# Normalising token blocks where they are read instead of where they are stored

## The chip, the core and the metric

One core of a Trainium2 chip runs the whole program. The metric is device time in microseconds from launch to end; the median of three runs of the kernel before is 2909.83 us (2909.57 to 2911.71). TensorE (PE) does the matmuls, VectorE (DVE) and ScalarE (ACT) the elementwise work and the evacuation of PSUM, GpSimd (POOL) some additions and a DMA queue, SyncE (SP) the main DMA queue. SBUF is the on-chip memory, PSUM holds the matmul results, HBM is off the chip.

## What is computed

Three layers on float32 data, 4 batches of 3072 tokens with 256 channels:

```python
X = np.fft.fft(np.fft.fft(x, axis=1), axis=2).real      # mixes tokens and channels
h = np.maximum(X @ w_in, 0.0)                           # 1024 wide
u, v = h[..., :512], h[..., 512:]
mu = np.mean(v, axis=-1, keepdims=True)
var = np.mean((v - mu) ** 2, axis=-1, keepdims=True)
v_n = (v - mu) / np.sqrt(var + 1e-06)                   # per token
v_s = np.einsum('ts,bsd->btd', w_spatial, v_n) + b_spatial[None, :, None]
y = (u * v_s) @ w_out                                   # 256 wide
gate = 1.0 / (1.0 + np.exp(-(y @ w_gate)))
out = (gate * (y @ w_val)) @ w_out2
```

The change concerns `v_n`: the scale 1/sqrt(var + 1e-6) and the shift -mu * scale of every token.

## The kernel before

Every float32 operand of a matmul is kept as a rounded high part and the remainder, the low part, and a product is three matmuls (`mm3`, L257 to L261: high x high, high x low, low x high).

**The front** (up to 321 us of the trace). Per batch, POOL folds the input `xt` by its symmetries (`fold_half`, `fold_x`, L371 and L372, `folds`), ACT and POOL split the folded tiles (`split_fold`, L254, L255), and PE transforms them along the tokens (`fft`, `psf`). The result, in four units a batch, feeds blocks of 128 tokens: `v_block` (a tile of 128 tokens x 512, and its mirror image) and `u_block` (128 channels of `u`). The order is written out by hand: a global `step` counts the blocks, 116 in all, 29 per batch, seven or eight per unit. A block's second matmuls come two steps after its first (`LAG = 2`), its third part one step later. Each unit needs a small tile `nt` that ACT makes from `nts` (`own_samples`, L592) at the last block of the unit before.

For a token tile `tv` ACT takes the Relu (L634, L640), DVE subtracts for the mirror image (`mirror`, L612) and takes the statistics (L642). After the last block of a unit come, one step each: `ln1` (aggregate, L673, L674), `root` (a square root on ACT, L677), `ln2` (L682 to L688: a Newton step, then `y`, the scale, and `nm`, the shift; `yp` lies in PSUM, in the pool of `lnb`), and three `norms` steps, which normalise two tiles each in place (`norm`, L693 on DVE or L697 on ACT by `NORM_ON`) and then store them to `v_d` in HBM (`store`, L703 to L709); unit 3 has one odd row in a tile of its own. A `u` tile goes from PSUM to `tu` (L660, L612) and to `u_d` (L665). The stores are issued on SP, those of the last batch on POOL. The tiles `tv` have 13 buffers, `tu` three.

At step 100 (`FIRST`) the program frees the tables of the front and starts to load blocks of the next stage (`start_a`), and at steps 106, 109, 113 and 115 (`NEXT`) it prepares the first four jobs (`prepare_next`).

**The spatial product** (321 to 1805 us). `w_spatial` times `v_n` is done with seven products of half-size blocks instead of eight (Strassen's scheme, `V_OF`, `W_OF`): for two pairs of batches `p`, seven products `i`, three column groups `c`, 42 leaves; each leaf has six steps `kp` of 24 matmuls. A job prepares one operand of one step: `load_job` brings one or two blocks of [128, 2, 512] from `v_d` or from the weights into `st` buffers (seven of them), `prepare_job` adds or subtracts the two where the scheme says so (L781, DVE), ACT casts the high part (L785), DVE takes the low part (L788, put off to the next job). There are 252 weight jobs and 84 token jobs; the token jobs of the next product run in the third leaf of the one before. `advance` prepares three steps ahead (`LEAD`) and loads two further.

**The second layer** (1805 us to the end) is not touched.

## Time and profile before

| what | value |
|---|---|
| median of the runs | 2909.83 us |
| span of the profiled execution | 2908.4 us |
| PE busy, of the span | 2832.1 us, 97% |
| DVE, ACT, POOL busy | 2039.4, 1341.2, 226.6 us |
| mean granted clock of TensorE, whole span | 0.991 |

The profile shows one execution. A busy PE is not PE at its peak, since overlapping matmuls count as one busy stretch; the number of matmuls in a stretch and the granted clock tell more. The time of a run is to be compared with other runs, the span with stretches of the same trace. Lines are those of the kernel before.

### The profile page before, as it was taken

How to read it: one execution, taken by the hardware profiler on the slowest of the kernel's cores; microseconds unless marked ns; L12 is line 12 of the kernel's file. 1: busy time of each engine (PE TensorE's matmuls, PEld its weight loads, DVE VectorE, ACT ScalarE, POOL GpSimd, SP SyncE). 2: the span in 40 equal slices, each digit the busy share in tenths (PEclk: the TensorE clock that was granted, in tenths of full speed). 3: DMA queues.
4: the chain of work that ended last, by engine and by line, in shares of the span. 5: the costliest groups of instructions: out<-in, count | busy, mean ns of one | idle time of the engine just before them, and what ended most of it. 6: DMA issues, size and time to landing. Idle time of an engine off the chain costs nothing.

```text
span 2908.4 us, 33957 instructions
## 1 busy us (share of the span) xinstructions
PE 2832.1 (97%) x12550; PEld 2355.8 (81%) x12550; DVE 2039.4 (70%) x2971; ACT 1341.2 (46%) x2151; POOL 226.6 (8%) x332
## 2 busy tenths in 40 slices
PE   5998799999999999999999999999999999999999
PEld 4887688888888888888888888888888888888887
DVE  7887775787766666577667476866677667766665
ACT  4888433233233232233223233666556556565655
POOL 2882100011100001000000000000000000000000
PEclk8999899999999999999999999999999999999999
DMA  6676866787756777587777485200000000000000
GB/s 227 241 257 237 320 236 202 267 312 264 261 200 212 263 248 255 177 287 256 246 257 242 147 278 169 82 34 29 30 3 27 30 30 30 15 15 30 29 15 15
DMA packets 148135, 470.75 MB, mean 162 GB/s; under 512 B 16753, under 2 KB 18289, under 8 KB 147584
## 3 DMA queue, kind: packets, MB, share of 16 engines
q1 hardware_dynamic: 140528, 434.88, 43.6%
q0 software_dynamic: 3984, 21.11, 1.8%
q10 hardware_dynamic: 3456, 12.58, 1.1%
q8 instruction: 98, 1.61, 0.2%
q14 instruction: 69, 0.57, 0.1%
HBM read 385.94 MB, written 82.58 MB: 161 GB/s over the span
## 4 chain that ended last, share of the span: by engine, by line
PE 92%; DVE 3%; ACT 2%; issue 1%; DMA 1%; POOL 0%; ACTq 0%; SPq 0%; DVEq 0%; POOLq 0%
PE bank L259 29%; PE bank L260 29%; PE bank L261 29%; DMA u_d<-tu 1%; PE psf L259 1%; PE psf L261 0%; PE psf L260 0%; PE psu L261 0%; PE psv L259 0%; PE psu L259 0%; PE psu L260 0%; PE psv L260 0%; PE psv L261 0%; DVE stats L642 0%; ACT tu L660 0%
## 5 line engine op out<-in xcount | busy, mean ns | idle before, releaser
L259 PE MATMUL bank<-wh,vh 128*128 128x512 f32 x2016 | 785.4, 390 | 6.7 <-DVE nm L688 6.7
L260 PE MATMUL bank<-wl,vh 128*128 128x512 f32 x2016 | 785.1, 389 | 0.0
L261 PE MATMUL bank<-wh,vl 128*128 128x512 f32 x2016 | 784.9, 389 | 0.0
L788 DVE TENSOR_TENSOR wl<-st,wh 128x1024 fp32r<-128x1024 f32 x252 | 311.3, 1235 | 430.9 <-ACT wh L785 427.6
L785 ACT CAST wh<-st 128x1024 fp32r<-128x1024 f32 x252 | 265.8, 1055 | 677.4 <-PE bank L261 442.5
L259 PEld LDWEIGHTS bank<-wh,vh 128*128 128x128 f32 x2016 | 379.0, 188 | 85.8 <-DVE nm L688 7.4
L261 PEld LDWEIGHTS bank<-wh,vl 128*128 128x128 f32 x2016 | 379.0, 188 | 79.0
L260 PEld LDWEIGHTS bank<-wl,vh 128*128 128x128 f32 x2016 | 379.0, 188 | 78.5
L781 DVE TENSOR_TENSOR st<-st 128x1024 f32<-128x1024 f32 x240 | 293.4, 1223 | 16.7 <-DMA st<-in_wt 11.6
L259 PE MATMUL bank<-x,wgh 128*128 128x512 f32 x673 | 262.4, 390 | 0.5 <-ACT t L1290 0.4
L1278 DVE TENSOR_TENSOR t<-t,bank 128x512 f32<-128x512 f32 x144 | 99.0, 688 | 233.5 <-PE bank L261 233.5
L260 PE MATMUL bank<-x,wgh 128*128 128x512 f32 x673 | 261.8, 389 | 0.0
L261 PE MATMUL bank<-x,wgl 128*128 128x512 f32 x673 | 261.8, 389 | 0.0
L1299 DVE TENSOR_TENSOR gl<-s,gh 128x512 fp32r<-128x512 f32 x288 | 199.5, 693 | 57.7 <-ACT gh L1297 44.4
L259 PE MATMUL bank<-gh,wv 128*128 128x512 f32 x576 | 224.2, 389 | 0.8 <-ACT gh L1292 0.8
L260 PE MATMUL bank<-gl,wv 128*128 128x512 f32 x576 | 224.2, 389 | 0.2 <-DVE gl L1299 0.2
L261 PE MATMUL bank<-gh,wv 128*128 128x512 f32 x576 | 224.1, 389 | 0.0
L1269 ACT ACTIVATE s<-s 128x512 f32<-128x512 f32 x144 | 91.1, 633 | 153.3 <-DVE s L1268 153.3
L259 PEld LDWEIGHTS bank<-x,wgh 128*128 128x128 f32 x673 | 126.3, 188 | 28.5 <-ACT s L1266 0.9
L1070 ACT COPY x<-bank 128x512 f32<-128x512 f32 x48 | 28.3, 589 | 259.2 <-PE bank L261 259.2
L261 PEld LDWEIGHTS bank<-x,wgl 128*128 128x128 f32 x673 | 126.4, 188 | 26.1
L260 PEld LDWEIGHTS bank<-x,wgh 128*128 128x128 f32 x673 | 126.4, 188 | 26.0
(232 smaller groups left out, 4467.8 us busy)
## 6 DMA issues: line engine op xcount, KB each, us to landing
st<-in_wt SPq DMA_DIRECT2D x432, 512.0 KB, 5.3
st<-v_d SPq DMA_DIRECT2D x144, 512.0 KB, 4.9
u<-u_d SPq DMA_DIRECT2D x96, 256.0 KB, 4.3
u_d<-tu SPq DMA_DIRECT2D x48, 384.0 KB, 3.3
v_d<-tv SPq DMA_DIRECT2D x69, 256.0 KB, 2.4
xt<-in_xh SPq DMA_DIRECT2D x24, 512.0 KB, 4.3
x_d<-x ACTq DMA_DIRECT2D x24, 512.0 KB, 2.7
raw<-x_d SPq DMA_DIRECT2D x24, 512.0 KB, 4.1
```

The costliest lines, as they stand in the source:

```text
L259: nc.tensor.matmul(out=ps, lhsT=w[0], rhs=x[0], start=first, stop=False, **kw)
L260: nc.tensor.matmul(out=ps, lhsT=w[0], rhs=x[1], start=False, stop=False, **kw)
L261: nc.tensor.matmul(out=ps, lhsT=w[1], rhs=x[0], start=False, stop=last, **kw)
L781: nc.vector.tensor_tensor(out=tiles[0], in0=tiles[0], in1=tiles[1], op=ALU.add if sign > 0 else ALU.subtract)
L785: nc.scalar.copy(hl[0], tiles[0])
L788: lows.append(lambda: nc.vector.tensor_tensor(out=hl[1], in0=tiles[0], in1=f(hl[0]), op=ALU.subtract))
L1070: nc.scalar.copy(side["x2"][:, o, :], ps)
L1269: nc.scalar.activation(s1, s1, AF.Sigmoid)
L1278: nc.vector.tensor_tensor(out=g["t2"], in0=g["t2"], in1=g["b"], op=ALU.add)
L1299: nc.vector.tensor_tensor(out=l, in0=s, in1=f(h), op=ALU.subtract)
```

## The change

Token tiles go to `v_d` as they are after the Relu, right after their statistics (`store` in `rest` and in `only`). `norm`, `norms`, `last_norm`, `NORM_ON` and the entries that followed `ln2` are gone. `ln2` writes scale and shift of all token tiles into one tile `ln_of` that stays in SBUF; the odd row of unit 3 is put there by an eight-byte DMA. In the spatial product `norm_job` applies scale and shift with two ACT operations per token job (to the second block where a job has two, with the shifts of both blocks combined), and `prepare_job` multiplies the first block by its scale in the same DVE operation that adds the second. `advance` issues `norm_job` for all jobs that are due before it prepares them. The pools change: `tv` from 13 buffers to nine, `tu` from three to five.

```diff
@@ -304,6 +304,9 @@
 
 
     r0, l0, f0 = ExitStack(), ExitStack(), ExitStack()
+    lnp = pool(ctx, "lnp", 1, "right")
+    ln_of = lnp.tile([P, B * 24, 2], F32, name="ln_of")
+    shifts = {}
     keep = pool(r0, "keep", 1, "right")
     pqp = pool(r0, "pqp", 2, "right")
     cst = pool(l0, "cst", 1)
@@ -580,8 +583,8 @@
         take_nyquist(*fft(fold_n, B, unit, 0, early=True), unit)
     s0.close()
     stp = pool(r0, "stp", 2, "right")
-    vp = pool(r0, "vp", 13, "right")
-    up = pool(r0, "up", 3, "right")
+    vp = pool(r0, "vp", 9, "right")
+    up = pool(r0, "up", 5, "right")
 
     lnb = ps_l.tile([P, 2, 8], F32, name="lnb")
     nt_of = {}
@@ -603,7 +606,7 @@
         tiles = {}
         stats = stp.tile([P, 7, 6], F32, name="stats")
         mv = stp.tile([P, 7, 2], F32, name="mv")
-        ve, sd, y, nm = (stp.tile([P, 7], F32, name=n) for n in ("ve", "sd", "y", "nm"))
+        ve, sd = (stp.tile([P, 7], F32, name=n) for n in ("ve", "sd"))
         yp = lnb[:, unit % 2, :]
 
 
@@ -622,7 +625,12 @@
                 tv = vp.tile([P, DH], F32, tag="tv", name="tv")
                 nc.scalar.activation(tv, ps, AF.Relu)
                 tiles[6] = tv
-                return lambda: lambda: nc.vector.bn_stats(stats[:, 6, :], tv)
+
+                def only():
+                    nc.vector.bn_stats(stats[:, 6, :], tv)
+                    store(6)
+
+                return lambda: only
             ev = stp.tile([P, DH], F32, tag="e", name="ev", bufs=4)
             nc.scalar.copy(ev, ps)
 
@@ -640,6 +648,7 @@
                 nc.scalar.activation(tv, tv, AF.Relu)
                 for sg in range(2):
                     nc.vector.bn_stats(stats[:, sg * 3 + m, :], tiles[sg * 3 + m])
+                    store(sg * 3 + m)
 
             return second
 
@@ -684,17 +693,17 @@
             stt(out=ve[:, a], in0=yp[:, a], scalar=-0.5, in1=ve[:, a], op0=ALU.mult, op1=ALU.mult)
             nc.vector.tensor_tensor(out=ve[:, a], in0=ve[:, a], in1=yp[:, a], op=ALU.mult)
             stt(out=yp[:, a], in0=ve[:, a], scalar=1.5, in1=yp[:, a], op0=ALU.add, op1=ALU.mult)
-            nc.vector.tensor_copy(y[:, a], yp[:, a])
-            stt(out=nm[:, a], in0=mv[:, a, 0], scalar=-1.0, in1=yp[:, a], op0=ALU.mult, op1=ALU.mult)
-
-        def norm(i):
-            tv = tiles[i]
-            if NORM_ON[i] != "a":
-                engines[NORM_ON[i]].tensor_scalar(
-                    out=tv, in0=tv, scalar1=y[:, i : i + 1], scalar2=nm[:, i : i + 1], op0=ALU.mult, op1=ALU.add
-                )
-            else:
-                nc.scalar.activation(tv, tv, AF.Identity, scale=y[:, i : i + 1], bias=nm[:, i : i + 1])
+            at = b * 24 + unit * 6
+            places = [(slice(0, 6), ln_of[:, at : at + 6, :])]
+            if nb == 7:
+                own = stp.tile([P, 1, 2], F32, name="own")
+                places.append((slice(6, 7), own))
+            for k, to in places:
+                nc.vector.tensor_copy(to[:, :, 0], yp[:, k])
+                stt(out=to[:, :, 1], in0=mv[:, k, 0], scalar=-1.0, in1=yp[:, k], op0=ALU.mult, op1=ALU.mult)
+            if nb == 7:
+                q = H - (R3 - P)
+                queue.dma_start(ln_of[0:1, at + 3 : at + 4, :], own[q : q + 1, :, :])
 
         def store(i):
             tv = tiles[i]
@@ -708,23 +717,12 @@
             else:
                 queue.dma_start(v_d[b][:, unit * 6 + i, :], tv)
 
-        def norms(i):
-            for k in (i, i + 3):
-                norm(k)
-            for k in (i, i + 3):
-                store(k)
-
-        def last_norm():
-            norm(6)
-            store(6)
-
         blocks = []
         for i in range(4):
             if i < nb - 3:
                 blocks.append(lambda i=i: v_block(i))
             blocks.append(lambda i=i: u_block(i))
-        after = [root, ln2] + [lambda i=i: norms(i) for i in range(3)] + ([last_norm] if nb == 7 else [])
-        return blocks, [ln1] + after
+        return blocks, [ln1, root, ln2]
 
 
     la, ls, ra, pa_ = ExitStack(), ExitStack(), ExitStack(), ExitStack()
@@ -773,14 +771,52 @@
                 tiles.append(st)
         staged[n] = tiles
 
+    def columns(p, block):
+        at = (2 * p + block[0]) * 24 + 12 * block[1]
+        return ln_of[:, at : at + 12, :]
+
+    def shift_of(p, i):
+
+        first, second, sign = V_OF[i]
+        if second is None:
+            return columns(p, first)[:, :, 1]
+        if (p, i) not in shifts:
+            shifts[p, i] = lnp.tile([P, 12], F32, name=f"shift{p}{i}")
+            nc.vector.tensor_tensor(
+                out=shifts[p, i],
+                in0=columns(p, second)[:, :, 1],
+                in1=columns(p, first)[:, :, 1],
+                op=ALU.add if sign > 0 else ALU.subtract,
+            )
+        return shifts[p, i]
+
+    def norm_job(n):
+
+        _, kind, key = jobs[n]
+        if kind == "v":
+            p, i, kp = key
+            first, second, _ = V_OF[i]
+            st, scale, shift = staged[n][-1], columns(p, second or first)[:, :, 0], shift_of(p, i)
+            for k in range(2):
+                at = slice(2 * kp + k, 2 * kp + k + 1)
+                nc.scalar.activation(st[:, k, :], st[:, k, :], AF.Identity, scale=scale[:, at], bias=shift[:, at])
+
     def prepare_job(n):
         _, kind, key = jobs[n]
         sign = (V_OF if kind == "v" else W_OF)[key[1]][2]
         tiles = staged.pop(n)
-        if sign:
-            nc.vector.tensor_tensor(
-                out=tiles[0], in0=tiles[0], in1=tiles[1], op=ALU.add if sign > 0 else ALU.subtract
-            )
+        op = ALU.add if sign > 0 else ALU.subtract
+        if sign and kind == "v":
+            p, i, kp = key
+            scale = columns(p, V_OF[i][0])[:, :, 0]
+            for k in range(2):
+                at = slice(2 * kp + k, 2 * kp + k + 1)
+                st = tiles[0][:, k, :]
+                nc.vector.scalar_tensor_tensor(
+                    out=st, in0=st, scalar=scale[:, at], in1=tiles[1][:, k, :], op0=ALU.mult, op1=op
+                )
+        elif sign:
+            nc.vector.tensor_tensor(out=tiles[0], in0=tiles[0], in1=tiles[1], op=op)
         hl = [A[kind].tile([P, 2, 512], F32R, tag=kind + i, name=kind + i) for i in "hl"]
         nc.scalar.copy(hl[0], tiles[0])
 
@@ -802,7 +838,11 @@
     def advance(step, loads):
 
         load_due(step + loads)
-        while state["prep"] < len(jobs) and jobs[state["prep"]][0] <= step:
+        due = state["prep"]
+        while due < len(jobs) and jobs[due][0] <= step:
+            norm_job(due)
+            due += 1
+        while state["prep"] < due:
             prepare_job(state["prep"])
             state["prep"] += 1
 
@@ -814,21 +854,20 @@
         load_due(1)
 
     def prepare_next():
+        norm_job(state["prep"])
         prepare_job(state["prep"])
         state["prep"] += 1
         load_job(state["load"])
         state["load"] += 1
 
     units = [(b, unit) for b in range(B) for unit in (3, 2, 0, 1)]
-    LAG, NORM_DVE = 1, (0, 1, 2, 3, 4, 5, 6)
-
 
 
     FOLDS, SPLITS, SPLIT_ON = (-3, 1, 4, 8, 13, 13), (17, 19, 23), "ppp"
     AT3, AT2, AT0, END0 = (26, 28), (2, 6), (11, 13), (10, 12)
     FIRST, NEXT = 100, (106, 109, 113, 115)
-    LAG, NORM_ON, NYQ = 2, "avavava", 4
-    engines = {"v": nc.vector, "p": nc.gpsimd}
+    LAG, NYQ = 2, 4
+    engines = {"p": nc.gpsimd}
     plan = {}
     folds_of, parts_of = {b: [] for b in range(B)}, {0: fold, B: fold_n}
     parts_of.update({b: [] for b in range(1, B)})
```

## Rows read from the trace of the kernel before

**Rows 1.** Busy by stretch: us of PE, PEld, DVE, ACT, POOL (instructions), clock, DMA, GB/s.

```profile
56.00:280.00 224.00, 206.27 (x1018) 185.20 (x1019) 182.97 (x455) 186.99 (x377) 150.59 (x233) 0.98 0.62 223
280.00:321.00 41.00, 22.21 (x89) 18.18 (x88) 29.62 (x80) 25.17 (x49) 13.61 (x25) 0.75 0.82 309
321.00:1805.00 1484.00, 1484.00 (x6539) 1228.33 (x6540) 1015.92 (x1147) 448.61 (x518) 48.57 (x54) 1.00 0.71 243
1805.00:2908.00 1103.00, 1097.94 (x4836) 906.93 (x4834) 762.10 (x1169) 659.37 (x1169) 0.00 (x0) 1.00 0.08 28
```

**Rows 2.** Waits of PE, 56 to 321 us: total us, times, longest us.

```profile
PE psv L620 <- ACT nt L592: 18.0, 7, 7.3
PE bank L259 <- DVE nm L688: 6.7, 1, 6.7
...
PE psu L259 <- ACT eu L654: 3.8, 3, 3.1
```

**Rows 3.** Busy time by stretch, the ten us ahead of a hot spot and in it.

```profile
90.00:100.00 10.00, 10.00 (x52) 9.04 (x51) 8.00 (x20) 9.49 (x20) 9.84 (x16) 1.00 0.88 319
100.00:110.00 10.00, 7.36 (x29) 6.21 (x28) 9.86 (x20) 9.81 (x20) 8.36 (x12) 0.83 0.41 160
```

**Rows 4.** Order of time, PE: start, us, instruction, idle before it and its releaser.

```profile
105.39 0.56 PE L620 MATMUL psv<-g,nt 128*128 128x512 f32 x1 [2.64 <-ACT nt L592]
...
165.85 0.50 PE L620 MATMUL psv<-g,nt 128*128 128x512 f32 x1 [2.65 <-ACT nt L592]
...
226.83 0.50 PE L620 MATMUL psv<-g,nt 128*128 128x512 f32 x1 [2.64 <-ACT nt L592]
```

**Rows 5.** Order of time, ACT, 89 to 105 us; first and last of five normalisations (L697).

```profile
89.39 0.82 ACT L697 ACTIVATE tv<-tv,nm,y 128x512 f32<-128x512 f32 x1
90.11 0.47 ACT L654 COPY eu<-psu 128x384 f32<-128x384 f32 x1
...
103.55 0.90 ACT L697 ACTIVATE tv<-tv,nm,y 128x512 f32<-128x512 f32 x1
...
104.62 0.72 ACT L592 ACTIVATE nt<-nt,masks 128x384 fp32r<-128x384 f32 x1
```

**Rows 6.** Chain of waits, 278 to 296 us: start, us, what.

```profile
281.51 10.75 DMA u_d<-tu
```

**Rows 7.** Order of time, ACT and POOL, 285 to 300 us.

```profile
292.33 0.48 ACT L660 COPY tu<-psu 128x384 f32<-128x384 f32 x1 [4.55 <-DMA u_d<-tu]
...
294.34 0.54 POOL L709 DMA_DIRECT2D v_d<-tv  x1 [8.04 <-ACT tv L697]
```

**Rows 8.** Groups by line and shape, 56 to 321 us: count | busy us, mean ns | idle before.

```profile
L697 ACT ACTIVATE tv<-tv,nm,y 128x512 f32<-128x512 f32 x50 | 41.5, 830 | 2.3 <-DVE nm L688 2.3
...
L693 DVE TENSOR_SCALAR tv<-tv,y,nm 128x512 f32<-128x512 f32 x46 | 37.7, 820 | 0.0
```

**Rows 9.** Groups by line and shape, DVE, 321 to 1805 us.

```profile
L781 DVE TENSOR_TENSOR st<-st 128x1024 f32<-128x1024 f32 x238 | 291.0, 1223 | 16.7 <-DMA st<-in_wt 11.6 <-DMA st<-v_d 4.5
...
L1023 DVE SCALAR_TENSOR_TENSOR g<-u,g 128x512 f32<-128x512 f32 x94 | 64.5, 686 | 0.8
...
L693 DVE TENSOR_SCALAR tv<-tv,y,nm 128x512 f32<-128x512 f32 x3 | 1.5, 543 | 0.0
```

**Rows 10.** Busy time by stretch, the last leaf of a block.

```profile
600.00:650.00 50.00, 50.00 (x222) 41.44 (x221) 48.07 (x53) 17.56 (x18) 3.50 (x4) 1.00 0.90 329
```

**Rows 11.** Order of time, ACT, 603 to 619 us.

```profile
604.97 1.06 ACT L785 CAST wh<-st 128x1024 fp32r<-128x1024 f32 x1 [3.44 <-PE bank L261]
...
615.85 1.06 ACT L785 CAST wh<-st 128x1024 fp32r<-128x1024 f32 x1 [2.58 <-PE bank L261]
```

**Rows 12.** Order of time, SP and POOL, one batch: loads of xt, last split.

```profile
116.33 1.41 SPq L366 DMA_DIRECT2D xt<-in_xh  x2
...
163.43 4.90 POOL L255 TENSOR_TENSOR fl<-fo,fh 128x1024 fp32r<-128x1024 f32 x2
...
176.07 0.88 SPq L366 DMA_DIRECT2D xt<-in_xh  x2
```

## The prediction

> **What bounds the kernel now.** Read the stages first, with the busy time of every engine by stretch [rows 1]. From 321 to 1805 us, the spatial product, PE is busy 1484.00 of 1484 us at full clock; from 1805 to the end, the second layer, 1097.94 of 1103. Both are PE from end to end: work taken from other engines there is worth nothing, and work added there costs nothing until PE runs out of prepared blocks. Only ahead of them does PE idle: 17.7 us of the 224 from 56 to 280, and 18.8 of the 41 from 280 to 321, 36.5 us in all. The front is therefore where time can come back. Next, what PE waited for [rows 2]: 18.0 of these us ended with ACT's `nt` (own_samples), 6.7 with the last of DVE's small operations on `nm`; the rest are short waits on ACT and DVE results, the longest 3.1.
>
> The `nt` waits are a queue, not a long operation. In the ten us from 100 PE issued 29 matmuls at a mean granted clock of 0.83, against 52 at 1.00 in the ten before [rows 3], and stood 2.64 us before the one matmul that needed `nt`; the same again at 165.85 and 226.83, once in each of the first three batches [rows 4]. ACT, 9.81 busy of those 10 us, had simply not come to `nt`: from 89.39 to the `nt` at 104.62 it had run five normalisations among its other work [rows 5]. The 23 matmuls missing are 23 x 10/52 = 4.4 us: the idle 2.6, and about 1.8 for matmuls at the lower clock behind it.
>
> The other big loss is where the last batch meets the first loads of the spatial product. The longest `nt` wait, 7.3 us, is there. The chain of waits leads from it to a store of `tu` that took 10.75 us to land [rows 6]: an ACT copy wanted that buffer (`up` has three) and stood 4.55 us; POOL, which issues the stores of this batch, stood 8.04 us at a `tv` store until ACT had normalised the tile [rows 7]. The stretch has 89 matmuls, at 5.2 a us 17 us of work in 41; of the loss, 18.8 is idle and about 5 slow clock (0.75) [rows 1, 3].
>
> **Removed from the front.** 100 normalisations (52 on ACT, 48 on DVE): the groups show 50 of 830 ns and 46 of 820 [rows 8], 41.5 us of ACT and 37.7 of DVE out of 265. ACT falls from 212 busy us to 171, DVE from 213 to 175, both well under PE's 228.5 [rows 1]. In a hot spot, ACT has to reach `nt` 2.64 us sooner; five normalisations less, at 0.72 us from one start to the next operation's (89.39 to 90.11, [rows 5]), are 3.6. I take the three hot spots back whole: 3 x 4.4 = 13.2 us. The short waits hang on chains of one ACT and one DVE operation that stay; outside the transition I take nothing for them.
>
> **Moved: the stores.** A token tile is stored right after its statistics instead of behind ln1, root, ln2 and a normalisation, six to nine steps later. Number, bytes and queues of the stores (SP for three batches, POOL for the last) stay. On SP they now stand ahead of some `xt` loads that they used to follow; they wait for a Relu that is already issued, so I price that at nothing. If that cover fails, a late load reaches the folding on POOL (rival 2). In the last batch POOL no longer stands at `tv` for a normalisation, and `up` has five buffers instead of three. With four u blocks in seven steps a `tu` buffer comes round after 8.75 steps instead of 5.25; a step is seven matmuls, 1.35 us at full pace, so 11.8 us against a slow landing of 10.75. I leave 1 us of the 7.3. `vp` falls from 13 to 9 tiles: six in seven steps, so 10.5 steps, 14 us, still above 10.75.
>
> **The transition in numbers.** 6.3 us from the first stall; 1.6 of the 3.1 (ACT's queue is shorter, DVE's work stays); 3.5 of the 5 of slow clock; and 1.7 of the final 6.7, for two or three normalisations of 0.5 to 0.8 us that leave the queues ahead of the last ln2, while Relu, statistics, aggregate, root and ln2 stay. Sum 13.1. DVE sets a floor there: 29.6 busy of 41 now, eight of 0.54 less [rows 1, 9], leaves 25 and some waiting; 41 - 13.1 = 27.9 just fits.
>
> **Added to the spatial product.** 84 token jobs get two ACT operations each, 168 x 0.83 = 139 us on an ACT that is busy 448.61 of 1484 [rows 1, 8]: hidden. Sixty jobs replace one addition over 1024 (1223 ns) by two multiply-adds over 512, nearest row 686 ns [rows 9]: from nothing (if they overlap as well as the long one) to 2 x 0.686 - 1.223 = 0.15 us each, 9 us at most, on a DVE busy 1016 of 1484. Ten additions of 12 columns for the shifts, eight small operations and four eight-byte DMAs for the odd row (0.54 us of POOL each at most, [rows 7]) lie beside other work; I take nothing, and the few us that they are in sum if none of it were hidden.
>
> What matters is the last third of each block of three leaves, where the next block's tokens are prepared too: DVE 48.07 of 50 us, DMA 0.90 [rows 10]. The cover is how early a job is ready. ACT's cast of a weight block still waits for PE there, 3.44 us at 604.97 and 2.58 at 615.85 [rows 11]. That wait ends when PE gives a buffer back, three steps before the cast's own block is used; a step is 24 matmuls of 1484/6539 us, 5.45 us, so from the 16.3 us the cast and the low part leave about 13. The wait shrinks by some 0.4 us a step, so 11 are left after six steps. A token job now also holds the loop for its two normalisations, 1.4 to 1.7 us, and up to 0.15 of DVE: if all of it added to the drift, 6 x 1.8 = 11 us, just the cover. Since ACT has about 3 us of waiting in each step I expect half of it and no stall: 0 us, with 0 to 4 us in each of ten blocks at the far end.
>
> **Sum.** 13.2 + 13.1 = 26.3 us off the profiled span of 2908.4, so 2882.1; the median of the runs is 1.4 above that span: 2883.5 us. A measurement of this kernel can tell 0.2%, 5.8 us, from no change.
>
> **Rivals.** (1) **PE alone sets the front.** Idle time and slow clock go, all but 5 us of the last chain: 36.5 + 3 x 1.8 + 5 - 5 = 42 us, 2868. For it: ACT and DVE lose some 40 us each. Against it: the short waits have causes that the change doesn't touch.
>
> (2) **The folding on POOL paces the batches.** `xt` is loaded at 116.33, folded until 163.43, and the next batch's load goes out at 176.07 [rows 12]: 47.1 of 59.7 us are POOL's, and the program needs some steps more before the next load. If these take 6 us, a batch can't go under 53. That leaves room for my 4.4 us, but an `xt` load delayed behind the new stores would use it up. Then only the transition gains, 10 to 13: 2898. Against it: DVE's normalisation takes 820 ns beside POOL's folds and 543 after them [rows 8, 9], so each may be slowing the other. The Trainium skill (SBUF — State Buffer, SBUF: two separate sides) says that DVE and GpSimd share a port pair which one instruction holds for its whole length, a DVE operation in a two-port mode among those that take it; by that rule POOL's folds would get shorter by up to 46 x 0.28 = 13 us, 4 a batch (an estimate), and this rival would fall. No row shows POOL alone, so its chance stays.
>
> (3) **The spatial product runs dry: slower.** Its place is the end of a block, its price the drift over the cover. If a token job costs the loop 3 us more a step (both normalisations, the load's landing that ACT now awaits ahead of the weight cast, buffers held so much longer), the drift is 18 us against 11: PE stands 6.5 us in ten blocks, 65 - 26 = 39 us lost, 2949. It begins at 1.8 us a step and outweighs the gain at about 2.3. Against it: ACT's waits in [rows 11].
>
> (4) **The wait only changes its name.** `nt` then waits for what DVE (9.86 busy of 10 in the hot spot, [rows 3]) gives to ACT, and the flood of loads still holds `tu`: within 5 us of before, 2907.
>
> **Chances.** Forecast (2873 to 2893) 0.56; rival 1 0.14; rival 2 0.16; rival 3 0.06; rival 4 0.08. The range, 2866 to 2902, holds the forecast and rivals 1 and 2 and leaves out 3 and 4. Faster by over 0.2%: 0.86; within: 0.08; slower: 0.06.
>
> **What would show it.** Right: no PE wait of 2 us before `nt` in the first three batches, the clock of the front near 1.00, POOL's stores no longer waiting for ACT, the spatial product's second bank starting near 295 us, and 1484 full us behind it. Wrong: PE waits on `psf` behind POOL's split (rival 2); PE idle inside the spatial product, ended by a block's low part (rival 3); `nt` still late (rival 4).

## The result, and the profile after

The changed kernel takes 2934.14 us (median of 4 runs, 2934.04 to 2935.72) against 2909.70 us for the kernel before (4 runs beside them): a ratio of 1.0084, 95% interval 1.0070 to 1.0099. It is slower by 24 us where 26 us of gain were forecast. The profiled execution has a span of 2933.9 us, 25.5 more than before.

Busy time by stretch of the changed kernel, the stretches of [rows 1] (the last one longer), in the same columns:

```profile
56.00:280.00 224.00, 210.60 (x1061) 189.65 (x1062) 163.39 (x450) 171.06 (x355) 158.02 (x253) 0.99 0.72 256
280.00:321.00 41.00, 32.77 (x129) 26.20 (x128) 35.21 (x62) 27.37 (x41) 6.18 (x12) 0.82 0.98 372
321.00:1805.00 1484.00, 1468.91 (x6428) 1213.14 (x6428) 1007.83 (x1193) 543.67 (x659) 46.13 (x48) 0.99 0.70 237
1805.00:2933.00 1128.00, 1123.69 (x4864) 913.56 (x4862) 767.87 (x1176) 661.46 (x1172) 0.00 (x0) 1.00 0.08 28
```

The front got what was expected: PE has 43 matmuls more from 56 to 280 and 40 more from 280 to 321. But the spatial stretch, full before, now has 15.1 us without a matmul, and the last one is longer although PE is as busy there as ever. Two points in PE's order of time give the loss by stage: the first matmul of the spatial product, and the last one of its last leaf, after which only the second layer follows.

```profile
291.66 0.63 PE L259 MATMUL bank<-wh,vh 128*128 128x512 f32 x1
...
1824.50 0.39 PE L261 MATMUL bank<-wh,vl 128*128 128x512 f32 x1
```

The same two in the kernel before:

```profile
312.66 0.63 PE L259 MATMUL bank<-wh,vh 128*128 128x512 f32 x1
...
1818.04 0.39 PE L261 MATMUL bank<-wh,vl 128*128 128x512 f32 x1
```

So the front is 21.0 us shorter (20.5 by the start of the second leaf, 334.0 against 354.5); from there to the end of the spatial product 27.0 us are lost; and the second layer, which no line of the change touches, takes 2933.9 - 1824.5 = 1109.4 us where it took 2908.4 - 1818.0 = 1090.4: 19.0 more. -20.5 + 27.0 + 19.0 = 25.5.

What PE waited for (total, times, longest), first from 56 to 321 us, where [rows 2] answers, then in the spatial product, where it had waited for nothing:

```profile
PE psv L623 <- ACT nt L595: 7.6, 6, 2.0
PE bank L259 <- DVE ln_of L703: 6.0, 1, 6.0
...
PE psu L259 <- ACT eu L663: 2.2, 2, 1.7
```

```profile
PE bank L260 <- DVE gl L1070: 15.1, 6, 3.3
```

The second is a new wait, six times, on `gl`: the low half of the gate.

**The wait on `gl`.** Products 5, 4, 2 and 6 end in an output: their banks are evacuated, multiplied with `u` into a gate `g`, and split into `gh` (ACT) and `gl` (DVE), while the next leaf already runs. Its four parts are made in steps 0 to 3 of that next leaf, and two small products in steps 4 and 5 use them (`second`). The last `gl` is put off until `second` begins, so on DVE it stands behind the conversions of step 4. In the kernel before, DVE and then PE at the first of these places, a leaf that began at 490.5 us:

```profile
492.77 1.23 DVE L788 TENSOR_TENSOR wl<-st,wh 128x1024 fp32r<-128x1024 f32 x1 [6.32 <-ACT wh L785]
...
496.84 1.22 DVE L781 TENSOR_TENSOR st<-st 128x1024 f32<-128x1024 f32 x1
497.98 1.22 DVE L788 TENSOR_TENSOR wl<-st,wh 128x1024 fp32r<-128x1024 f32 x1
...
518.80 0.69 DVE L1031 TENSOR_TENSOR gl<-g,gh 128x512 fp32r<-128x512 f32 x1
```

```profile
519.95 0.39 PE L260 MATMUL bank<-gl,woh 128*128 128x512 f32 x1
```

`gl` is finished at 519.49 and PE uses it at 519.95: 0.46 us of room, and no wait, so no view of waits names it. The six places are the third leaves of products 5, 4 and 2 in both pairs of batches, where the tokens of the next product are prepared beside the weights. At four of them the room is 0.46 or 0.47 us; at the two of product 4 it is used up already (`gl` ends 0.06 us before its use, and these leaves take 38.3 us instead of 38.1). In the other leaves behind an output the last `gl` lies ready 4 to 10 us before its use. The changed kernel at the same leaf, which begins at 470.0 us; ACT, DVE and PE:

```profile
471.21 1.52 ACT L802 ACTIVATE st<-st,shift,ln_of 128x512 f32<-128x512 f32 x2 [0.42 <-ACT x L1109]
472.63 1.04 ACT L821 CAST wh<-st 128x1024 fp32r<-128x1024 f32 x1
```

```profile
472.06 1.46 DVE L815 SCALAR_TENSOR_TENSOR st<-st,ln_of 128x512 f32<-128x512 f32 x2 [7.25 <-ACT st L802]
473.70 1.22 DVE L824 TENSOR_TENSOR wl<-st,wh 128x1024 fp32r<-128x1024 f32 x1 [0.19 <-ACT wh L821]
...
501.26 0.68 DVE L1070 TENSOR_TENSOR gl<-g,gh 128x512 fp32r<-128x512 f32 x1
```

```profile
502.00 0.50 PE L260 MATMUL bank<-gl,woh 128*128 128x512 f32 x1 [2.37 <-DVE gl L1070]
```

DVE's first low part comes 3.70 us after the leaf's start instead of 2.27, because ACT's scale and shift of the token block, 1.42 us from start to start, now stands ahead of the weight cast. From there to `gl` it is 27.56 us instead of 26.03: four multiply-adds on this way take 1.33 to 1.65 us each up to the next operation, an addition 1.14. Late by 1.4 + 1.5 with 0.46 of room: 2.5, and PE stood 2.37. The time behind it counts too. The 20 us from 500 to 520 us, changed kernel, then the one with an earlier `gl` (below):

```profile
500.00:520.00 20.00, 18.00 (x72) 14.74 (x73) 17.53 (x21) 8.77 (x11) 0.00 (x0) 0.91 0.94 336
```

```profile
500.00:520.00 20.00, 20.00 (x90) 16.56 (x89) 15.92 (x19) 8.89 (x11) 0.00 (x0) 1.00 0.92 328
```

18 matmuls are missing, at 226.7 ns 4.1 us: the wait and the lower clock after it (0.91 in the mean of the 20 us; from 503.10 to 506.00 us it is 0.50, the lower of the two levels, and a matmul takes 0.63 us instead of 0.39). The leaf goes from 38.1 to 42.4 us, and six such leaves, at 42.3 to 43.3, are 26 of the 27 us.

**The second layer.** PE's groups by line and shape, from the end of the spatial product to the end; kernel before, then changed:

```profile
L259 PE MATMUL bank<-x,wgh 128*128 128x512 f32 x669 | 260.6, 390 | 0.5 <-ACT t L1290 0.4
...
L261 PE MATMUL bank<-gh,wv 128*128 128x512 f32 x576 | 224.1, 389 | 0.0
```

```profile
L259 PE MATMUL bank<-x,wgh 128*128 128x512 f32 x669 | 263.3, 394 | 0.4 <-ACT t L1329 0.4
...
L261 PE MATMUL bank<-gh,wv 128*128 128x512 f32 x576 | 226.6, 393 | 0.0
```

Same instructions, same counts, same waits, granted clock 1.00 in both, and the matmuls 2 to 4 ns longer. In 500 us in the middle of the layer, kernel before, then changed:

```profile
1900.00:2400.00 500.00, 500.00 (x2208) 414.15 (x2207) 342.62 (x526) 299.16 (x530) 0.00 (x0) 1.00 0.07 26
```

```profile
1900.00:2400.00 500.00, 500.00 (x2169) 407.53 (x2168) 337.48 (x518) 294.33 (x522) 0.00 (x0) 1.00 0.07 26
```

From start to start a matmul takes 226.7 ns in the mean of this stretch before, and 230.7 after. What differs is where tiles lie. The new pool `lnp` takes 1408 bytes of each partition: `ln_of` 768, and ten shift tiles of 48 bytes, 64 apart. It is opened first on its side of SBUF, so the two pools of the second half on that side, `cp` (the second layer's output weights `wv`, the last leaf's gate `tail`, whose tiles later hold inputs of the layer, and one input tile, `x7`) and `gp` (gates, evictions, `gh`, `gl`), lie 1408 bytes lower: in the built program `cp` starts at byte 178688 instead of 180096. The pools on the other side (`vr`, `wr` with the split weights `wgh`, `wgl`, and `xq` with the other seven input tiles `x`) stay. Before, the start of every one of them was 128 bytes over a multiple of 256; after, those of `cp` and `gp` are multiples of 256.

### The profile page after: what moved, and what is told of

The parts are those of the page before. It is cut to its first block, busy times and chain, and to the rows that moved or that the text cites. A ratio compares the mean times of both kernels' runs of the same rounds, so it can differ in the third digit from the quotient of the medians.

```text
span 2933.9 us, 34266 instructions
## 1 busy us (share of the span) xinstructions
PE 2855.7 (97%) x12550; PEld 2358.3 (80%) x12550; DVE 2023.8 (69%) x3001; ACT 1424.8 (49%) x2267; POOL 224.3 (8%) x333
## 4 chain that ended last, share of the span: by engine, by line
PE 87%; DVE 6%; issue 3%; ACT 3%; DMA 1%; POOL 0%; ACTq 0%; DVEq 0%; POOLq 0%
PE bank L261 28%; PE bank L259 28%; PE bank L260 28%; DVE vl L824 1%; DVE st L815 1%; DVE g L1062 0%; PE psf L259 0%; ACT st L802 0%; DVE gl L1070 0%; DVE wl L824 0%; DMA st<-v_d 0%; PE psf L261 0%; PE psf L260 0%; DVE st L819 0%; PE psv L260 0%
## 5 line engine op out<-in xcount | busy, mean ns | idle before, releaser
L819 DVE TENSOR_TENSOR st<-st 128x1024 f32<-128x1024 f32 x180 | 219.5, 1220 | 5.9 <-DMA st<-in_wt 5.7
```

The lines of the kernel that those rows point to most:

```text
L819: nc.vector.tensor_tensor(out=tiles[0], in0=tiles[0], in1=tiles[1], op=op)
```

## The experiments

Two theories came out of the traces. **A:** the conversions of the token blocks make `gl` late (A1: ACT's scale and shift; A2: DVE's multiply-add). **C:** the second layer is slower because of the places of its tiles. The rivals: that loads or the moved tiles cause the waits in the spatial product (B), and that something else of the change slows the second layer (D). Where one time is given it is that of one execution; the kernel before took 2907.7 to 2913.9 us beside these runs. The second layer's length is the span less the start of the last leaf's last matmul.

**Which of the added steps delays `gl`.** Three kernels, each without something of the change:

```diff
 def norm_job(n):
-        if kind == "v":
+        if kind == "none":      # first and second kernel
 def prepare_job(n):
-        if sign and kind == "v":
+        if sign and kind == "none":      # first and third kernel
```

> The changed kernel with both of its new steps in the spatial stage left out: no ScalarE scale and shift on a token block, and the plain add or subtract of two blocks in place of the combined multiply-add, so the spatial product works on tokens that are not normalised; everything ahead of that stage is as in the changed kernel. Theory A (the added steps delay the low half of the gate, which the second product of products 5, 4 and 2 waits for): the six waits of a bank on the gate's low half, 15.1 us in 6 with the half-speed clock behind them, vanish and the stage from the first leaf to its last weight-block matmul goes from 1532.8 us back to about 1505.3; the time is 2934 less 27, about 2907. Theory B (the stage is slower because of where its tiles lie or of the loads, not of the two steps): the six waits stay and the time is within 5 us of 2934. The second layer, 1109.4 us in the changed kernel, stays there by both.

Measured: 2886.8 us. No wait on `gl`, the spatial product without a loss, as theory A has it. The time is 20 us below what was expected, and the second layer shows why: 1090.2 us. Without the scale and shift the shift tiles aren't made either, so `lnp` has 768 bytes, and `cp` and `gp` lie three times 256 lower. That was an unplanned first test of theory C. The second leaf starts at 331.2 us, against 332.4 to 334.0 in the four kernels that have both added steps and the changed front (the changed kernel is the latest of them): the added steps also cost the transition something, 1.2 to 2.7 us.

> The changed kernel without its ScalarE scale and shift of token blocks (left out of the computation), with the combined multiply-add on VectorE kept. Theory A1 (ScalarE's two added instructions, which stand ahead of a step's first cast and wait for the loaded block, start the step's chain of conversions 1.43 us late): the six waits on the gate's low half fall from 15.1 us to under 3 us, and the time to about 2910. Theory A2 (VectorE's pair of combined instructions, 1.33 to 1.46 us against 1.14 for the one it replaced, five steps in a row, is what uses up the 0.5 us of room): the waits stay above 5 us and the time above 2920. Theory B (neither): 2934 within 3 us.

Measured: 2891.5 us, again with 768 bytes and a second layer of 1090.2 us. PE's waits in the spatial product:

```profile
PE bank L260 <- DVE gl L1070: 2.1, 6, 0.7
```

As A1 expects. The multiply-add alone uses up the 0.46 us and a little more. Its price is in DVE's order of time: the pair starts at 474.84, the next instruction at 476.17,

```profile
474.84 1.41 DVE L815 SCALAR_TENSOR_TENSOR st<-st,ln_of 128x512 f32<-128x512 f32 x2
476.17 1.22 DVE L824 TENSOR_TENSOR wl<-st,wh 128x1024 fp32r<-128x1024 f32 x1
```

1.33 us, where the addition of before took 1.14 (496.84 to 497.98 above): 0.19 more.

> The changed kernel with ScalarE's scale and shift kept, and the combined multiply-add replaced by the plain add or subtract of before (the scale of the first of two blocks is left out of the computation). Theory A1 (ScalarE's added instructions alone make the low half of the gate late): the six waits stay near 9 us or more, 1.4 us of the 2.4 each plus the clock behind it, and the time stays above 2922. Theory A2 (VectorE's longer pair makes it): the waits go below 4 us and the time to about 2910. If both are needed to use up the room, this run and the one without ScalarE's step are both near 2910.

Measured: 2933.4 us, and

```profile
PE bank L260 <- DVE gl L1070: 16.3, 6, 3.1
```

So A1: ACT's two instructions at the head of the chain delay it whether DVE adds or multiplies and adds; with the plain addition DVE waits for ACT instead. B is out by two runs: the first of these three kernels has the loads of the changed one and no wait on `gl`, and the kernel before with its tiles moved (the next run below) has the places of the changed one, and no wait on `gl` either.

**Whether place alone slows the second layer.** In the kernel before, with no instruction added:

```diff
+    padp = pool(ra, "padp", 1, "right")
+    padp.tile([P, 352], F32, name="pad")
     cp = pool(ra, "cp", 1, "right")
```

> The kernel before with one unused tile of 1408 bytes a partition opened just ahead of the second half's pools on their side of SBUF, so that the tiles of the gate and of the second layer lie where the changed kernel has them; no instruction is added. Theory C (the second layer's matmuls are slower because of where their tiles lie): the pitch of the second layer's matmuls goes from 226.8 to 231 ns, the second layer from 1090.4 to about 1109 us, the time to 2909.8 plus 19, about 2929. Theory D (it is something else of the changed kernel, such as more to store or other DMA traffic): 2910 within 2 us.

Measured: 2930.3 us; second layer 1109.5 us; 500 us of it:

```profile
1900.00:2400.00 500.00, 500.00 (x2169) 407.51 (x2168) 337.51 (x518) 294.66 (x522) 0.00 (x0) 1.00 0.07 26
```

The count of the changed kernel, from the kernel before. Theory D is out.

**Mending each, and both.** Three kernels made from the changed one (`kp == 4` is the fifth step of a leaf):

```diff
     lnp = pool(ctx, "lnp", 1, "right")
+    lnp.tile([P, 32], F32, name="pad")            # first and third
...
         for kp in range(6):
+            if kp == 4 and before is not None:
+                finish_gate(before[2])            # second and third
             advance(6 * n + kp + LEAD, 2)
```

> The changed kernel with one unused tile of 128 bytes a partition beside its scales and shifts, so that the second half's tiles on that side of SBUF lie 1536 bytes below where the kernel before has them, a multiple of 512, instead of 1408. Theory C2 (what slows the second layer is the offset of those tiles against the other tiles by a part of 512 bytes): its matmuls go back from 231 to 226.8 ns of pitch, the second layer from 1109.4 to about 1090.5 us, the time to 2934 less 19 to 21, about 2914. Theory C3 (the offset counts by some larger period, or any move of that size does it): 2934 within 2 us. The six waits on the gate's low half, 15.1 us, stay by both.

Measured: 2912.9 us, second layer 1090.2 us, six waits on `gl` of 14.2 us together: C2.

> The changed kernel with the last low half of the gate taken by VectorE ahead of step 5 of the next leaf instead of inside the second product, where it stood behind that step's conversions; no instruction is added. Theory A (the waits come from that instruction's place behind ScalarE's scale and shift and the conversions): the six waits of 15.1 us fall under 2 us, the stage from the first leaf to its last weight-block matmul goes from 1532.8 to about 1506, the time to 2934 less 26, about 2908, the second layer staying at 1109. Rival (VectorE has no room in that step whatever the order, so that the wait moves to the step's conversions): the time stays above 2925 and waits of a bank on the low halves of token or weight blocks take the place of the six.

Measured: 2908.5 us; no wait on `gl` and none in its place; second layer 1109.4 us: theory A, its rival is out. DVE takes the last two `gl` together and goes on with the same work behind them:

```profile
495.19 1.46 DVE L1070 TENSOR_TENSOR gl<-g,gh 128x512 fp32r<-128x512 f32 x2
496.56 1.22 DVE L819 TENSOR_TENSOR st<-st 128x1024 f32<-128x1024 f32 x1
```

> Both edits in the changed kernel: the unused tile of 128 bytes and the earlier low half of the gate. If the two losses are separate and add up, as theories A and C2 have it: 2934 less 26 less 20, about 2888, faster than the kernel before by 0.7%, with the second layer at 1090.5 us and the stage ahead of it at about 1506. If only one of them is mended, about 2908 to 2914; if neither, 2934.

Measured: 2888.48 us (4 runs, 2887.53 to 2888.92) against 2911.02 (7 runs); ratio 0.9923, 95% interval 0.9906 to 0.9939. The losses are separate and add up, and this version is 0.8% faster than the kernel before. Its stretches:

```profile
321.00:1790.00 1469.00, 1469.00 (x6483) 1216.38 (x6482) 1017.51 (x1206) 550.71 (x668) 46.11 (x48) 1.00 0.71 239
1900.00:2400.00 500.00, 500.00 (x2207) 414.03 (x2206) 344.80 (x530) 298.07 (x529) 0.00 (x0) 1.00 0.06 23
```

PE is full from end to end, with ACT's 168 added operations still there.

> The kernel before with the last low half of the gate taken ahead of step 5 of the next leaf, the edit that took 26 us off the changed kernel; no instruction is added. Theory A (in the kernel before that low half came about 0.5 us before it was needed, and the product never waited for it): nothing to gain, 2910 within 3 us. Rival (the edit gains by itself, something else in the stage being shortened): below 2900.

(The same two lines in the kernel before.) Measured: 2908.8 us against 2907.8 beside it: nothing, as A has it. The edit only gives back what the change had taken.

**The buffers in the front.**

```diff
-    vp = pool(r0, "vp", 9, "right")
-    up = pool(r0, "up", 5, "right")
+    vp = pool(r0, "vp", 12, "right")
+    up = pool(r0, "up", 3, "right")
```

> The changed kernel with the front's buffers for u tiles back at three (and twelve for token tiles), as the kernel before had three; all else as changed. It splits the front's gain: the first three batches gained 11.7 us by 246 us, the transition to the spatial product 9.3 more. Theory T1 (the transition's gain comes from the five buffers, the prediction's 7.3 us stall behind a store of a u tile that takes long to land): the longest wait before `nt` near 280 us is back at 5 to 7 us, the spatial product's first bank starts at 297 to 299 us instead of 291.7, and the time is 2939 to 2941. Theory T2 (it comes from ScalarE and VectorE having no normalisations left there, and from the earlier stores): the first bank starts within 1.5 us of 291.7 and the time is within 3 us of 2934. By both the first three batches keep their 11.7 us.

Measured: 2933.0 us; the first bank starts at 293.9 us, the second leaf at 335.0 (334.0 with five buffers); the wait near 280 us:

```profile
PE psv L623 <- ACT nt L595: 9.1, 6, 3.6
```

Between the two, nearer to T2, though the first bank meets neither theory's mark: the stall that was 7.3 us before is 3.6 with three buffers and 2.0 with five. Of the transition's gain 1 to 2.5 us are the buffers' (the first bank starts at 291.4 to 291.8 us and the second leaf at 332.4 to 334.0 in the four kernels with five); the rest is put down to the queues without normalisations and to the earlier stores, which no run separates.

**Which places count.** All in the kernel before; an unused tile ahead of a pool moves it and those opened after it on its side.

```diff
+    padp = pool(ra, "padp", 1, "right")           # all but the x and the gp kernel
+    padp.tile([P, 32], F32, name="pad")           # [P, 16] for 64 bytes
     cp = pool(ra, "cp", 1, "right")
+    padq = pool(ra, "padq", 1, "right")           # gp alone; and cp alone, where gp comes to 256
+    padq.tile([P, 32], F32, name="padq")
     gp = pool(ra, "gp", 1, "right")
...
+        A["pad"] = pool(la, "padl", 1)            # all of the second half
+        A["pad"].tile([P, 32], F32, name="padl")
         A["v"] = pool(la, "vr", 7)
...
+            padx = pool(lx, "padx", 1)            # x; and cp, gp and x
+            padx.tile([P, 32], F32, name="padx")
             Bp["xq"] = pool(lx, "xq", 1)
```

> The kernel before with an unused tile of 128 bytes a partition ahead of the second half's pools on their side of SBUF, which moves them by 128 bytes where the earlier unused tile moved them by 1408 (768, as in the runs without the shift tiles, left the second layer at 389 ns a matmul). Theory C4 (the offset counts by a period of 256 bytes; 1408 is 5 x 256 + 128, 768 is 3 x 256): the second layer is as slow as with 1408, 231 ns of pitch, and the time about 2929. Theory C5 (a period of 512 or 1024 bytes: 1408 is 384 over, 128 is not): 2909 within 2 us, or a slowdown of another size.

> The kernel before with both pools of the second half moved by 64 bytes, where 128 and 1408 made the second layer some 19 us longer and, in runs of the changed kernel, 768 and 1536 did not. Theory C4 (only offsets by a multiple of 256 bytes leave the matmuls at 226.8 ns): a slow second layer, 1100 us or more, 2918 or more. Theory C13 (it is 128 bytes modulo 256 alone that slows it, as two tiles then meet): 2909 within 3 us.

> The kernel before with the unused 128 bytes placed between its two pools of the second half, so that only the pool of the gate, its evictions and the split gated rows (gh, gl, s, t) moves by 128 bytes, while the pool of the second layer's output weights and of the last leaf's gate stays. Theory C6 (the slow matmuls come from ScalarE and VectorE working in that moved pool while PE reads the others, or from gh and gl against the weights): the second layer stays near 231 ns a matmul, about 2928. Theory C7 (the moved output weights and the last leaf's tiles are the cause): 2909 within 3 us, or only the matmuls on gh and gl slower.

> The kernel before with the pool of the second layer's output weights and of the last leaf's gate (tail) moved by 128 bytes and the pool of the gate and its evictions by 256, which amounts to leaving it: the complement of the run that moved the latter alone and took 2921.5 us of span. Theory C10 (each pool slows the matmuls by itself, and the losses add up): the second layer loses about 19 - 13 = 6 us against 1090.4, and the time is about 2915, with the matmuls on x and tail slower more than those on gh and gl. Theory C11 (the losses don't add up, either move brings most of it): 2920 or more. Theory C12 (the gate's pool is all of it): 2909 within 3 us.

> The kernel before with the second layer's input tiles x moved by 128 bytes and everything else in its place. With both pools moved too the matmuls on x took 395 to 397 ns and the second layer 1117 us. Theory C14 (a matmul slows when its own moving operand lies 128 bytes off): the matmuls on x go to 393 or more and those on gh, gl and tail stay at 389; second layer 8 to 15 us longer, 2917 to 2925. Theory C15 (it takes the moved pools of VectorE's and ScalarE's tiles): 2909 within 3 us.

> The kernel before with both pools of the second half moved by 128 bytes, as in the run that took 2928, and with the second layer's input tiles x moved by 128 bytes as well (the split weights of the second layer stay). Theory C8 (it is the offset between x and the moved pools that counts): back to 226.8 ns of pitch and about 2910. Theory C9 (it is the address itself, or the offset against the weights): still near 2928, or slower.

> The kernel before with every tile of its second half moved by 128 bytes: the pools of prepared tokens and weights (which also hold the second layer's split weights), the staging tiles and the x tiles in their place, and both pools on the other side. All their distances stay as they are up to multiples of 256 bytes. Theory C16 (what counts is the distance between the tiles that PE and the other engines read at one time): 226.8 ns of pitch, second layer 1090 us, 2909 within 3 us. Theory C17 (it is the address itself, 128 over a multiple of 256 being the good one): the second layer is as slow as with the moved parts, 2926 to 2936, and the spatial stage, whose tiles had their old places in every other run, may be slower too.

Measured, with the runs above:

| what is moved, by how many bytes | second layer, us | matmuls, 1900 to 2400 us | time, us |
|---|---|---|---|
| nothing | 1090.4 | 2208 | 2909.7 |
| `cp` and `gp`, 1408 | 1109.5 | 2169 | 2930.3 |
| `cp` and `gp`, 128 | 1109.5 | 2168 | 2928.1 |
| `cp` and `gp`, 64 | 1111.1 | 2165 | 2930.1 |
| `gp` alone, 128 | 1103.5 | 2180 | 2923.3 |
| `cp` alone, 128 (`gp` 256) | 1110.4 | 2164 | 2931.7 |
| `x` alone, 128 | 1105.8 | 2180 | 2927.0 |
| `cp`, `gp` and `x`, 128 | 1117.1 | 2152 | 2935.2 |
| all of the second half, 128 | 1090.4 | 2207 | 2913.7 |
| changed kernel, 1536 in all | 1090.2 | 2207 | 2912.9 |

The two ends of it, `cp`, `gp` and `x` moved, then every tile of the second half:

```profile
1900.00:2400.00 500.00, 500.00 (x2152) 404.83 (x2151) 335.74 (x513) 291.68 (x518) 0.00 (x0) 1.00 0.07 26
```

```profile
1900.00:2400.00 500.00, 500.00 (x2207) 414.04 (x2206) 343.46 (x529) 299.48 (x531) 0.00 (x0) 1.00 0.07 26
```

Theory C16 holds: a common move of everything costs the layer nothing, a move of some tiles against the others costs 13 to 27 us, unless it is a multiple of 256 bytes (768 and 1536). So C4 over C5 and C13, and C11 over C10 and C12: either pool brings a loss of its own, and they don't add up. C8 fell, C9 holds: `x` moved along with the two pools made it worse; the split weights had stayed behind. C6 and C7 are right in a part each: `gp` alone costs 13.1 us, neither the whole loss nor nothing, and it is `gh` and `gl` against the weights that slow (below). C14 is half right, C15 is out: with `x` moved alone the layer takes 15.4 us more and the matmuls on `x` 392 to 395 ns, but those on `gh` and `gl` also rise, to 390 and 391. (The kernel with everything moved loses 3.5 us elsewhere, before its second leaf, which starts at 358.0 us. That start lies between 351.4 and 355.9 in the other kernels made from the one before; no cause is read from it.)

**Whose reads they are.** The trace holds all 12550 matmuls in the order of the program, so each can be set beside the places of its two operands in the built program: the moving tile, and the weights. With `gp` alone moved, `gh` and `gl` start at a multiple of 256 bytes, and everything else that PE reads 128 bytes over one. From 1900 to 2800 us the 1426 matmuls whose moving tile lies so against its weights take 231.9 ns from start to start, the first, second and third behind each run of them 231.7, 232.5 and 230.8, and the 1782 others 226.7, as before, although DVE and ACT work in moved tiles beside these too. A piece of it:

```profile
2001.46 0.40 PE L259 MATMUL bank<-gh,wv 128*128 128x512 f32 x1
...
2002.85 0.39 PE L259 MATMUL bank<-tail,wg 128*128 128x512 f32 x1
...
2003.55 0.39 PE L259 MATMUL bank<-x,wgh 128*128 128x512 f32 x1
...
2004.23 0.39 PE L259 MATMUL bank<-x,wgh 128*128 128x512 f32 x1
...
2005.59 0.40 PE L259 MATMUL bank<-gh,wv 128*128 128x512 f32 x1
```

Six matmuls on `gh` and `gl` take 1.39 us, 232 ns each; the three on `tail` behind them 0.70 us, 233 each; then nine on `x` 2.04 us, 227 each. Nor does it need another engine at the time. With `cp`, `gp` and `x` moved, a stretch in which DVE, ACT, POOL and the DMA queues do nothing, and the first and the fourth matmul of it:

```profile
2233.23:2233.95 0.72, 0.72 (x5) 0.58 (x4) 0.00 (x0) 0.00 (x0) 0.00 (x0) 1.00 0.00 0
```

```profile
2233.22 0.40 PE L260 MATMUL bank<-x,wgh 128*128 128x512 f32 x1
...
2233.93 0.39 PE L260 MATMUL bank<-tail,wgh 128*128 128x512 f32 x1
```

That is 237 ns each. The 55 matmuls of this kernel from 1830 to 2900 us that have no instruction of DVE, ACT or POOL and no DMA packet within 0.1 us take 240.8 ns; the 57 such ones of the kernel before take 226.5.

So it is PE's own reads that count: the remainders by 256 of a matmul's moving tile and of its weights, and of those of the matmuls just before it. That also covers matmuls that seem untouched: in the changed kernel, those between two others on the same unmoved `x`, with unmoved weights, go from 226.8 to 230.8 ns (437 and 434 of them, 1900 to 2800 us). How long it lasts behind a mismatch differs, three matmuls with `gp` alone moved, up to nine with `x` alone. Why it lasts, and what in PE's reading takes the time, no run shows.

## Why the prediction was wrong

**What bounds the kernel: right.** PE bounds the two long stages, and the front's idle time could be won.

**The front: right in mechanism, 6 us too large.** Forecast 26.3 us; measured 21.0 at the first bank and 20.5 at the second leaf. The first three batches, with the three hot spots, gave 11.7 of 13.2: the matmul on `spc` that starts at 270.21 us before starts at 258.53 after. Ten us ahead of the first and in it, where [rows 3] answers, and PE's waits there, where [rows 4] answers:

```profile
90.00:100.00 10.00, 10.00 (x53) 9.15 (x52) 7.70 (x19) 8.54 (x19) 9.84 (x17) 1.00 0.71 253
100.00:110.00 10.00, 8.90 (x43) 7.35 (x42) 6.43 (x16) 9.73 (x21) 8.37 (x11) 1.00 0.76 288
```

```profile
103.35 0.51 PE L623 MATMUL psv<-g,nt 128*128 128x512 f32 x1 [0.95 <-ACT nt L595]
...
160.43 0.50 PE L623 MATMUL psv<-g,nt 128*128 128x512 f32 x1 [0.93 <-ACT nt L595]
...
217.65 0.50 PE L623 MATMUL psv<-g,nt 128*128 128x512 f32 x1 [0.94 <-ACT nt L595]
```

The clock stays at 1.00 there. ACT's queue is still the limit (9.73 busy of 10), so 0.94 us of each 2.64 remain. The transition gave 9.3 of 13.1. Term by term: the first stall 5.3 (7.3 to 2.0) for 6.3; the wait on `eu` 1.4 (3.1 to 1.7) for 1.6; the clock 0.82 for a forecast that took 3.5 of the 5 us back from 0.75; the last wait 0.7 (6.7 to 6.0) for 1.7. What the forecast put at nothing is the added steps on the first blocks: 1.2 to 2.7 us by the kernel without them. The reason given for the first stall was mostly wrong: three `up` buffers leave 3.6 us of it, not 7. The bank after the last wait was to start near 295 us; it starts at 299.14, from 320.83:

```profile
299.14 0.79 PE L259 MATMUL bank<-wh,vh 128*128 128x512 f32 x1 [6.00 <-DVE ln_of L703]
```

**The stores: right in the main.** POOL, which had stood 8.04 us for ACT at a store [rows 7], stands 3.36 us at most for ACT in the same 15 us (285 to 300), so it still waits, but shorter; the forecast had it no longer wait. Rival 2, POOL's folding, didn't decide: the hot spots gave their gain. The sentence there on the port that DVE and GpSimd share, by the Trainium skill (SBUF — State Buffer, SBUF: two separate sides), gave an estimate of up to 13 us of shorter folds. The trace doesn't bear out that size: a fold of 128x512 goes from 1330 to 1296 ns, and POOL's six costliest groups of additions, from 56 to 300 us, from 102.6 to 99.9 us in sum.

**The spatial product: wrong, 0 forecast, 27 lost.** The costs of the operations were nearly right: 1.4 to 1.7 us for the scale and shift (measured 1.42), 0 to 0.15 for the multiply-add (0.19). The step that failed is "The cover is how early a job is ready": the cover was worked out for weight and token jobs, some 11 us, and held, since PE never waited for a block. With it fell the sentence that added work "costs nothing until PE runs out of prepared blocks": PE never ran out of them and lost 27 us. The gate's low half goes through the same two queues, has 0.46 us at four of the six places and none at two, and was not looked at: [rows 10] and [rows 11] are of the third leaf of product 1, which has no output and so no gate. A view of waits can't show a consumer that just doesn't wait; the order of time can.

**Rival 3** (the product runs dry) had the direction and a chance of 0.06, but another mechanism: a drift over a whole block that begins at 1.8 us a step and at 3 us costs 6.5 us in each of ten blocks (its own figures, 18 us of drift against 11, give 7, and 2954 instead of 2949). What came is one late operation in six leaves, 4.3 us each, without any drift.

**The second layer: wrong, 0 forecast, 19 lost.** That the change doesn't touch it was taken to mean that it keeps its time, so the sum has no term for it. What was left out is where `lnp` lies: it moves every tile behind it, and against the tiles on the other side, which stay, that cost 4 ns a matmul in the mean. No row of the trace of before could give the price.

With both mended the kernel takes 2888.5 us, 5 above the predicted time. It gains 22.5 us where 26.3 were forecast; the other 1.2 of the 5 come from the kernel before, which took 2911.0 us beside these runs.

## What to carry to other kernels

Before work is added to a queue "with room", list every consumer fed from it, also those that never wait, and take from the order of time how long each result lies ready before its use; the smallest of these is the room, here 0.46 us at best and not 11. Where it is too small, take the late result out from behind the new work: one moved call gave 26 us back. And look where a new long-lived tile pushes the others: pad its pool so that the tiles that PE reads together keep their distances up to a multiple of 256 bytes, or a stage that nobody touched may slow by 2%.

## What the runs showed of the hardware

A matmul's pitch, the time from its start to the next one's, depends on the places of the tiles in SBUF: 226.7 ns in the second layer when all tiles start at the same remainder by 256 bytes (128 in the kernel before, 0 in the one with everything moved), 229.5 to 232.5 in the mean when some are 64 or 128 bytes off (2180 to 2152 matmuls in 500 us), at the same granted clock of 1.00 and without a wait in the trace. With `gp` alone moved the loss sits in the matmuls whose moving tile and weights differ in that remainder, and in the three behind each run of them (230.8 to 232.5 ns; all others 226.7). Matmuls of the spatial product, whose moving tiles and weights kept their distances from one another in all these runs, didn't slow by more than 0.2% (leaves of 32.6 to 32.7 and 38.1 to 38.3 us between the first and the last, in the kernels made from the one before). The Trainium skill (SBUF — State Buffer, SBUF: two separate sides) has PE, ACT and DVE's own port pair waiting for nobody and names the pair shared with GpSimd as the only place where engines meet. The trace agrees so far as POOL does nothing in the second layer (0.00 us) and matmuls are as slow with DVE, ACT and the DMA queues idle around them (240.8 against 226.5 ns): the cost is in PE's own reads.
